# Down projection, token pairs 2 to 7: the second product moved to the end of the pair, and y's second half loaded in pieces of 128 tokens

## The chip, the cores and the metric

The kernel runs on one core of a Trainium2 chip. The metric is the device time of one execution in microseconds. Three executions of the kernel before took 781.5, 782.49 and 782.85 us; their median, 782.49 us, is the time before.

## The reference

A transformer block with modulation: a linear attention part and a gated feed-forward part, each with a residual. The change lies in the last matmul of the second, `@ w_down`.

```python
def _B_ref(x, w_gate, w_up, w_down):
    return _gelu(x @ w_gate) * (x @ w_up) @ w_down
x = A_x
mod = (_silu(c) @ w_mod).reshape(c.shape[0], 6, 1, -1)
...
x = x + ga * _A_ref(h, A_wqkv, A_wo)
h = _layernorm(x, axis=-1) * (1 + cb) + sb
x = x + gb * _B_ref(h, B_w_gate, B_w_up, B_w_down)
```

x has 2048 tokens of 1024 values, w_gate and w_up are 1024x3584, w_down is 3584x1024, all bf16. In the kernel y stands for `_gelu(x @ w_gate) * (x @ w_up)`, and the final line is out = x1 + gb * (y @ w_down), with x1 the result of the attention part.

## The kernel before, in words

**Recording and order.** Each instruction is recorded by `sch.op` or `sch.dma` with the byte ranges that it reads and writes in SBUF and in PSUM; from these the recorder derives what it must wait for, engine by engine, and emits semaphore waits. At the end `sch.reorder` rearranges the streams of VectorE (DVE), ScalarE (ACT) and GpSimd (POOL) by a table of costs and due times. The streams of TensorE (PE) and of SyncE (SP, which issues nearly all DMAs) keep the order in which they are written. DMAs of SP share 8 semaphore lanes in turn, and one waits for the one 8 before it.

**The down projection.** The 2048 tokens go in 8 pairs of token tiles, j = 0 to 7, of 2 x 128 tokens. The loop `for j in range(1, NP)` (L1917) handles j = 1 to 7, and `lastj` marks j = 7. For one pair, y (256 tokens by 3584) is held as two halves of the summation, `YL[0]` (`lo`) and `YL[1]` (`hi`), each of 14 chunks (k) of 128 by 256 tokens; w_down's columns are two halves of 512 (`BXT` and `STT`). The 2x2 block product (token tile s by column half c) is computed with seven products in place of eight, from sums and differences of the blocks. Each product is 14 matmuls of 128x128 by 128x512 (`dprod`, L1655, all issued on L1647):

- P1 and P2 take y's first token tile as it was loaded, in bf16: P1 from `YL[0]`, P2 from `YL[1]`.
- P5, P6, P7, P3 and P4 take sums of y blocks, in `XS[0]` or `XS[1]` (fp32r), and sums of weight blocks, prepared earlier (`TT`).
- `a_sum(i, k0, k1)` (L1627) makes the sums in two parts of 7 chunks: 0 writes XS[0] for P5, 1 writes XS[1] for P6, 2 writes XS[0] for P7, 3 writes XS[1] for P3 (it reads `YL[1]`, tokens 0 to 127), all on VectorE; 4 copies `YL[1]`, tokens 128 to 255, to XS[0] for P4, on ScalarE.

**PSUM.** Four banks for a pair, and the other four for the next (t = j % 2): `BA`, `BE`, `BB`, `BC` (L1406).

- P1 starts BA; `dpcp` (L1678, ScalarE) copies BA to BB; P2 adds to BA, which then holds output block 0 (tile 0, columns 0 to 511).
- P5 starts BE; `descp` (ScalarE) copies BE to `ES[0]` in SBUF.
- P6 adds to BB; `dpadd(j, BC)` (L1686, VectorE) writes BC = BB + ES[0]; P3 adds to BC: output block 1.
- P7 adds to BB; `dpadd(j, BE)` writes BE = BB + ES[0]: output block 2.
- P4 adds to BB: output block 3.

The order of TensorE in a pair is P1, P5, P6, P2, P7, P3, P4.

**Leaving PSUM.** `devac(j, n)` (L1706) finishes output block n: one VectorE op multiplies the bank by gb (L1714), one adds x1 from a slot in SBUF (L1715), and SP writes the slot to the output (L1716). `x1_load(j, n)` (L1699) has loaded that slot; there are 7 slots, and block n of pair j uses slot (4j+n) % 7.

**Loads of y.** `y_load(j, l, k0, k1, s0, s1)` (L1621) loads half l of pair j from DRAM (`scr_y`), chunks k0 to k1 and tokens s0 to s1 (all 256 unless given). Each half has a single buffer, so a load waits for every reader of what it overwrites. In SP's order of pair j come y_load(j+1, 0) after a_sum 2, and y_load(j+1, 1) in two parts of 7 chunks, each behind its part of a_sum 4.

Of the kernel before, what the change touches and what calls it, by code (L numbers as in the profile page):

```python
# [10 lines left out]
P = 128  # L11
# [53 lines left out]
NKP = NFP  # L65
NST = 14
# [284 lines left out]
def bass_adaLN_cond__linear_attn_block__geglu_ffn__prompt_kernel(  # L351
# [18 lines left out]
    with ExitStack() as es:  # L370
# [175 lines left out]
        def r_yl(l, k0=0, k1=NKP, s0=0, s1=256):  # L546
            if s1 - s0 == 256:
                return [(OFF_YL[l] + k0 * 512, OFF_YL[l] + k1 * 512, f"yl{l}")]
            return [(OFF_YL[l] + k * 512 + s0 * 2, OFF_YL[l] + k * 512 + s1 * 2, f"yl{l}") for k in range(k0, k1)]

        def r_xq(i, k0, k1):
            return [(OFF_XS[i] + k0 * 512, OFF_XS[i] + k1 * 512, f"xs{i}")]

        def r_bx(k, l0=0, l1=2):
            return [(PB[k] + l0 * 1024, PB[k] + l1 * 1024, f"bx{k}")]
# [4 lines left out]
        def r_bt(k, i):  # L560
            return [(PT[k][i], PT[k][i] + 2048, f"bt{k}_{i}")]

        def r_slot(i):
            return [(OFF_SLOT[i], OFF_SLOT[i] + 1024, f"x1s{i}")]
# [11 lines left out]
        def pr(b):  # L576
            return [(b * 2048, (b + 1) * 2048)]

        def PS(b, c0=0, c1=512):
            return ps_all[:, b * 512 + c0: b * 512 + c1]  # L580
# [1040 lines left out]
        def y_load(j, l, k0=0, k1=NKP, s0=0, s1=256):  # L1621
            sch.dma(Q, lambda e: e.dma_start(YL[l][:, k0:k1, s0:s1], scr_y[j // 4, :, j % 4, l, k0:k1, s0:s1]), wr=r_yl(l, k0, k1, s0, s1),
                    deps=o_y[j // 4], note=f"yl{j}.{l}.{k0}.{s0}", overwrite_ok=True)
# [19 lines left out]
        def dmm(b, fresh, lhs, rhs, note, c0=0, c1=512):  # L1643
            pend_ = None
            n = len(lhs)
            for i, ((l_, rl), (r_, rr)) in enumerate(zip(lhs, rhs)):
                pend_ = sch.op(T, lambda e, l_=l_, r_=r_, i=i: e.matmul(PS(b, c0, c1), l_, r_, start=fresh and i == 0, stop=i == n - 1, skip_group_check=True),  # L1647
                               rd=rl + rr, pwr=(pr(b) if i == 0 else ()), note=f"{note} {i}", overwrite_ok=True)
            if pend_ is not None:
                pset_writer(b, pend_)  # L1650

        def ya(l, s, k):
            return YL[l][:, k, s * P:(s + 1) * P], r_yl(l, k, k + 1, s * P, (s + 1) * P)

        def dprod(j, i, k0, k1, n=512):  # L1655
            t, ks = j % 2, range(k0, k1)
            if i in (1, 2):
                lhs = [ya(i - 1, 0, k) for k in ks]
                rhs = [(BXT[k][:, i - 1, :], r_bx(k, i - 1, i)) for k in ks]
            else:  # L1660
                xi, ti = {5: (0, 0), 6: (1, 1), 7: (0, 2), 3: (1, 3), 4: (0, 4)}[i]
                lhs = [(XS[xi][:, k, :], r_xq(xi, k, k + 1)) for k in ks]
                rhs = [(TT[k][ti][:, 0:n], r_bt(k, ti)) for k in ks]
            b = {1: BA, 2: BA, 5: BE, 6: BB, 7: BB, 4: BB, 3: BC}[i] + t
            dmm(b, i in (1, 5) and k0 == 0, lhs, rhs, f"down j{j} P{i}", 0, n)
# [12 lines left out]
        def dpcp(j):  # L1678
            t = j % 2
            sch.op(A, lambda e: e.activation(PS(BB + t), PS(BA + t), ACTF.Copy), prd=pr(BA + t), pwr=pr(BB + t), note="pcp")  # L1680

        def descp(j):
            t = j % 2
            sch.op(A, lambda e: e.activation(ES[0][:, :], PS(BE + t), ACTF.Copy), prd=pr(BE + t), wr=r_2k(OFF_ES[0], "es0"), note="escp")

        def dpadd(j, dst):  # L1686
            t = j % 2
            sch.op(V, lambda e: e.tensor_tensor(PS(dst + t), PS(BB + t), ES[0][:, :], ALU.add), prd=pr(BB + t), rd=r_2k(OFF_ES[0], "es0"),
                   pwr=pr(dst + t), note="padd")

        def t4_gate(k):
            sch.op(V, lambda e: e.tensor_tensor(TT[k][4][:, :], TTF[k][4][:, :], GB16[:, 0:512], ALU.mult), rd=r_bt(k, 4) + R_GB16, wr=r_bt(k, 4), note=f"t4g{k}")

        def tok(j):
            return (j // 4) * 8 + 2 * (j % 4)
# [3 lines left out]
        def x1_load(j, n):  # L1699
            s, c = TORD[n]  # L1700
            i = (4 * j + n) % 7
            c_ = tok(j) + s
            sch.dma(Q, lambda e: e.dma_start(SLT[i][:, :], scr_x1[c_, :, c * 512:(c + 1) * 512]), wr=r_slot(i), deps=[o_x1[c_ // 4]],
                    note=f"x1l{c_}.{c}", overwrite_ok=True)

        def devac(j, n, c0=0, c1=512, b=None):  # L1706
            s, c = TORD[n]
            i, c_ = (4 * j + n) % 7, tok(j) + s
            if b is None:
                b, p0, p1 = ((BA, BC), (BB, BE))[s][c] + j % 2, c0, c1  # L1710
            else:
                p0, p1 = 0, c1 - c0
            rng = [(OFF_SLOT[i] + c0 * 2, OFF_SLOT[i] + c1 * 2, f"x1s{i}")]
            sch.op(V, lambda e: e.tensor_tensor(PS(b, p0, p1), PS(b, p0, p1), GB16[:, c * 512 + c0:c * 512 + c1], ALU.mult), prd=pr(b), pwr=pr(b), rd=R_GB16, note=f"x2a {j}.{n}")  # L1714
            sch.op(V, lambda e: e.tensor_tensor(SLT[i][:, c0:c1], PS(b, p0, p1), SLT[i][:, c0:c1], ALU.add), prd=pr(b), rd=rng, wr=rng, note=f"x2b {j}.{n}")  # L1715
            sch.dma(Q, lambda e: e.dma_start(out_v[:, c_, c * 512 + c0:c * 512 + c1], SLT[i][:, c0:c1]), rd=rng, note=f"out{c_}.{c}.{c0}")  # L1716

        def rest_gate(j):
            b, i = BB + j % 2, (4 * j + 3) % 7
            sch.op(V, lambda e: e.tensor_tensor(PS(b), PS(b), GB16[:, 0:512], ALU.mult), prd=pr(b), pwr=pr(b), rd=R_GB16, note="u3g")  # L1720
            for h in range(2):
                d, p0, p1 = BB + (j + h) % 2, h * 256, h * 256 + 256
                sch.op(V, lambda e, d=d, p0=p0, p1=p1: e.tensor_tensor(PS(d, p0, p1), PS(b, p0, p1), SLT[i][:, p0:p1], ALU.add),
                       prd=pr(b), pwr=pr(d), rd=r_slot(i), note=f"u3x{h}")
# [107 lines left out]
        for n in range(7):  # L1832
            i, j = divmod(n, 2)
# [31 lines left out]
        H = (NST + 1) // 2  # L1865
        NP = S // 256

        def halves(i):
            a_sum(i, 0, H)
            a_sum(i, H, NST)  # L1870
# [46 lines left out]
        for j in range(1, NP):  # L1917
            lastj = j == NP - 1
            dprod(j, 1, 0, NST)
            dpcp(j)  # L1920
            if j == 1:
                devac(0, 0)
            else:
                halves(0)
                halves(1)
                devac(j - 1, 3)
            x1_load(j, 3)
            dprod(j, 5, 0, NST)
            descp(j)
            halves(2)  # L1930
            if lastj:
                for k in range(H, H + 4):
                    t4_gate(k)
            if not lastj:
                y_load(j + 1, 0)
            if j == 1:
                devac(0, 1)
            dprod(j, 6, 0, NST)
            dpadd(j, BC)
            halves(3)  # L1940
            if j == 1:
                devac(0, 2)
            dprod(j, 2, 0, NST)
            devac(j, 0)
            if lastj:
                for k in range(H + 4, NST):
                    t4_gate(k)
            if not lastj:
                x1_load(j + 1, 0)
            dprod(j, 7, 0, NST)  # L1950
            dpadd(j, BE)
            a_sum(4, 0, H)
            if not lastj:
                y_load(j + 1, 1, 0, H)
            a_sum(4, H, NST)
            if not lastj:
                y_load(j + 1, 1, H, NKP)
            devac(j, 2)
            if j == 1:
                devac(0, 3)  # L1960
            if not lastj:
                x1_load(j + 1, 1)
            if lastj:
                dprod(j, 3, 0, H - 1)
                dprod(j, 4, 0, H)
                rest_gate(j)
                dprod(j, 3, H - 1, NST)
                devac(j, 1)
                for h in range(2):
                    last_half(j, h)  # L1970
                continue
            dprod(j, 3, 0, NST)
            devac(j, 1)
            if not lastj:
                x1_load(j + 1, 2)
            dprod(j, 4, 0, NST)


        sch.reorder(mark[0], mark[1], (DVE_, ACT_, POOL_), {id(x4_op): 8.0})
# [73 lines left out]
```

## Time and profile before

| | |
|---|---|
| median of three runs | 782.49 us |
| the profiled execution: time / span | 781.51 us / 779.5 us |
| TensorE busy | 769.2 us, 99% of the span |
| VectorE, ScalarE, GpSimd busy | 656.8, 340.1, 47.6 us |
| down projection, one pair (j = 4, P1 to P1) | 22.04 us: TensorE busy 21.94, VectorE 15.25, ScalarE 3.09 |
| granted TensorE clock | 1.00 |
| y loads of 448 KB, from issue to landing | 4.1 us (median of 12) |
| output writes of 128 KB, from issue to landing | 1.7 us (median of 31) |

The profile is of one execution. Its span runs from the first instruction to the last; its time also holds what lies around them. PE is TensorE's matmuls and PEld its weight loads, which run under the matmul before. A matmul's recorded duration is longer than its distance to the next, since matmuls are pipelined; start-to-start distances are the better measure. A row "A <- B: 20.1, 11, 2.2" says that engine and line A stood idle until B released it, 20.1 us in 11 waits, the longest 2.2. Lines of a timeline give the start and the duration in us, the engine, the line, what is written and read, how many instructions are merged in the row, and in brackets the idle time ahead and what ended it.

### The profile page before, as it was taken

The numbers are of one execution on the slowest core, as the hardware profiler recorded it, in microseconds if no ns is written. First come the engines' busy times: TensorE is split into PE (matmuls) and PEld (weight loads), VectorE is DVE, ScalarE is ACT, GpSimd is POOL, SyncE is SP. The second block draws the span as 40 slices with busy tenths as digits, with TensorE's granted clock in tenths as the row PEclk, the third lists the DMA queues.
The fourth block names the chain that finished last, engine by engine and source line by source line (L and its number), as shares of the span: only waits on it lengthen the run. The fifth ranks groups of instructions, "written<-read, shape, count | busy, mean of one in ns | idle before, by whom it ended". The sixth has DMA issues, their size and how long they took to land.

```text
span 779.5 us, 10982 instructions
## 1 busy us (share of the span) xinstructions
PE 769.2 (99%) x3784; PEld 503.2 (65%) x3847; DVE 656.8 (84%) x1121; ACT 340.1 (44%) x566; POOL 47.6 (6%) x126
## 2 busy tenths in 40 slices
PE   8999999999999999999999999999999999999998
PEld 4444445666445676767676776767676676677766
DVE  6699989797698978897899989898889987676777
ACT  2497732211474577766654445444543211111111
POOL 2031300000230011100000000000000000000000
PEclk9999999999999999999999999999999999999999
DMA  9789759826697077847436475646545553344341
GB/s 290 250 170 250 158 93 250 230 69 123 137 247 190 28 206 239 226 116 185 132 111 172 126 207 188 198 118 195 148 123 151 157 171 119 120 142 135 115 135 40
DMA packets 209846, 125.92 MB, mean 162 GB/s; under 512 B 70528, under 2 KB 199424, under 8 KB 209792
## 3 DMA queue, kind: packets, MB, share of 16 engines
q1 hardware_dynamic: 209632, 125.16, 59.9%
q8 instruction: 30, 0.49, 0.3%
q14 instruction: 24, 0.20, 0.1%
q10 hardware_dynamic: 160, 0.07, 0.0%
HBM read 88.35 MB, written 23.22 MB: 143 GB/s over the span
## 4 chain that ended last, share of the span: by engine, by line
PE 91%; DVE 3%; SPq 3%; DMA 2%; issue 1%; ACT 0%; DVEq 0%; ACTq 0%
PE ps_all L1434 45%; PE ps_all L1647 23%; PE ps_all L944 7%; PE ps_all L1264 7%; PE ps_all L893 5%; PE ps_all L908 4%; SPq L631 1%; SPq L636 1%; DVE acc L844 1%; DMA wk<-in_A_wqkv_dram 1%; DVE acc L830 1%; DMA h1T<-xh 0%; DMA scr_row<-qt 0%; DMA mtb<-mb 0%; DVE w L1201 0%
## 5 line engine op out<-in xcount | busy, mean ns | idle before, releaser
L1434 PE MATMUL ps_all<-ss,tp 128*128 128x512 f32 x896 | 214.7, 396 | 0.0
L1434 PEld LDWEIGHTS ps_all<-ss,tp 128*128 128x128 f32 x896 | 168.1, 188 | 38.3 <-DVE ps_all L1446 0.6
L1647 PE MATMUL ps_all<-bt,xs 128*128 128x512 f32 (+1 forms) x552 | 130.2, 393 | 0.1
L1647 PEld LDWEIGHTS ps_all<-bt,xs 128*128 128x128 f32 x552 | 102.8, 188 | 23.3 <-issue 0.5
L1446 DVE TENSOR_TENSOR ps_all<-ps_all,es 128x512 f32<-128x512 f32 x112 | 77.6, 697 | 38.0 <-PE ps_all L1434 34.3
L1451 ACT ACTIVATE ge<-ps_all 128x512 f32<-128x512 f32 x112 | 64.1, 598 | 90.0 <-DVE ps_all L1446 46.1
L1402 DVE TENSOR_TENSOR tp<-wt 128x512 fp32r<-128x512 bf16 x112 | 74.4, 686 | 2.1 <-DMA wt<-in_B_w_gate_dram 1.5
L1455 DVE TENSOR_TENSOR yr<-ge,ps_all 128x512 bf16<-128x512 f32 x112 | 74.3, 683 | 1.5 <-PE ps_all L1434 0.9
L1402 DVE TENSOR_TENSOR tp<-wt,tp 128x512 fp32r<-128x512 bf16 x112 | 74.3, 685 | 0.0
L893 PE MATMUL ps_all<-wk,h1T 128*128 128x512 bf16 x239 | 55.3, 379 | 1.4 <-DVE h1T L757 0.8
L944 PE MATMUL ps_all<-h1T,wq 128*128 128x512 bf16 x256 | 56.7, 379 | 0.0
L1264 PE MATMUL ps_all<-w,pq 128*128 128x512 bf16 x252 | 55.9, 379 | 0.3
L1434 PE MATMUL ps_all<-ar,tp 128*128 128x512 f32 x224 | 55.3, 389 | 0.0
L882 ACT ACTIVATE eb<-ps_all 128x512 f32<-128x512 f32 x64 | 36.4, 594 | 39.0 <-PE ps_all L893 16.8
L1647 PE MATMUL ps_all<-bx,yl 128*128 128x512 bf16 x217 | 52.2, 380 | 0.8
L1434 PE MATMUL ps_all<-h20a,wt 128*128 128x512 bf16 x210 | 47.9, 379 | 0.9
L1434 PE MATMUL ps_all<-h21a,wt 128*128 128x512 bf16 x210 | 47.8, 379 | 1.0
L1434 PEld LDWEIGHTS ps_all<-ar,tp 128*128 128x128 f32 x224 | 42.0, 188 | 8.7
L1443 ACT ACTIVATE es<-ps_all 128x512 f32<-128x512 f32 x56 | 33.5, 600 | 30.8 <-PE ps_all L1434 30.8
L1440 ACT ACTIVATE ps_all<-ps_all 128x512 f32<-128x512 f32 x56 | 32.6, 582 | 30.6 <-PE ps_all L1434 30.3
L944 PEld LDWEIGHTS ps_all<-h1T,wq 128*128 128x128 bf16 x256 | 24.9, 98 | 30.0
L1264 PEld LDWEIGHTS ps_all<-w,pq 128*128 128x128 bf16 x256 | 24.8, 98 | 30.1 <-issue 0.5
(143 smaller groups left out, 880.8 us busy)
## 6 DMA issues: line engine op xcount, KB each, us to landing
wt<-in_B_w_gate_dram SPq DMA_DIRECT2D x28, 512.0 KB, 4.1
wt<-in_B_w_up_dram SPq DMA_DIRECT2D x28, 512.0 KB, 5.1
scr_y<-yr SPq DMA_DIRECT2D x56, 256.0 KB, 4.9
yl<-scr_y SPq DMA_DIRECT2D x8, 896.0 KB, 4.7
wmst<-in_w_mod_dram SPq DMA_DIRECT2D x6, 1024.0 KB, 6.8
yl<-scr_y SPq DMA_DIRECT2D x12, 448.0 KB, 4.1
wmq<-in_w_mod_dram SPq DMA_DIRECT2D x8, 512.0 KB, 7.6
rb<-scr_rd SPq DMA_DIRECT2D x32, 128.0 KB, 3.0
```

The lines of the kernel that those rows point to most:

```text
L882: sch.op(A, lambda e: e.activation(EB[i][:, :], PS(bank), ACTF.Exp), prd=pr(bank), wr=rng, note=f"{note}.exp")
L893: o = sch.op(T, lambda e, dc=dc: e.matmul(PS(bank), H1[sg][:, ci, dc, :], W_[:, dc, jg * 512:(jg + 1) * 512], start=(dc == 0), stop=(dc == ...
L944: o = sch.op(T, lambda e, dc=dc: e.matmul(PS(b), WQ[:, dc, qc * P:(qc + 1) * P], H1[sg][:, :, dc, :], start=(dc == 0), stop=(dc == NDC - 1 ...
L1264: last[half] = sch.op(T, lambda e, g=g, half=half: e.matmul(PS(b0 + half), PQ[sg][:, g, ci * P:(ci + 1) * P], W2[:, g, half * 512:(half + ...
L1402: sch.op(V, lambda e, t=t: e.tensor_tensor(TP[k][:, t, :, :], in0[:, t, :, :], in1[:, t, :, :], ALU.subtract), rd=r0[t:t + 1] + (r1[t:t + ...
L1434: o = sch.op(T, lambda e, l_=l_, r_=r_, dc=dc: e.matmul(PS(b), l_, r_, start=fresh and dc == 0, stop=dc == ND2 - 1, skip_group_check=True) ...
L1440: sch.op(A, lambda e: e.activation(PS(BB + t), PS(ba + t), ACTF.Copy), prd=pr(ba + t), pwr=pr(BB + t), note="pcp")
L1443: sch.op(A, lambda e: e.activation(ES[t][:, :], PS(be + t), ACTF.Copy), prd=pr(be + t), wr=r_2k(OFF_ES[t], f"es{t}"), note="escp")
L1446: sch.op(V, lambda e: e.tensor_tensor(PS(dst + t), PS(BB + t), ES[t][:, :], ALU.add), prd=pr(BB + t), rd=r_2k(OFF_ES[t], f"es{t}"), pwr=pr ...
L1451: sch.op(A, lambda e: e.activation(GE[i][:, :], PS(b), ACTF.Gelu_apprx_tanh), prd=pr(b), wr=r_2k(OFF_GE[i], f"ge{i}"), note="gelu")
L1455: sch.op(V, lambda e: e.tensor_tensor(YR[:, 2 * (v % 2) + l, h * SGW:(h + 1) * SGW], GE[i][:, :], PS(b + 1), ALU.mult), rd=r_2k(OFF_GE[i], ...
L1647: pend_ = sch.op(T, lambda e, l_=l_, r_=r_, i=i: e.matmul(PS(b, c0, c1), l_, r_, start=fresh and i == 0, stop=i == n - 1, skip_group_check ...
```

## The change

For j = 1 to 6 (the second to the seventh pair):

- P2 moves from between P6 and P7 to the end of the pair, behind P4. On TensorE the order is then P1, P5, P6, P7, P3, P4, P2, followed by the next pair's P1. Both P2 and P1 are bf16 products.
- `devac(j, 0)`, which needs P2, moves into the next pair, behind `devac(j, 3)` and ahead of `x1_load(j+1, 3)`, which uses the slot that it frees.
- y's second half of the next pair is loaded in three DMAs in place of two: tokens 128 to 255 at the two old places, tokens 0 to 127 (all 14 chunks) at the end of the pair, behind P2, which reads the old ones.

Pair 7 keeps P2 and its devac where they were, and so does pair 0, which lies outside the loop.

```diff
@@ for j in range(1, NP)
                 halves(0)
                 halves(1)
                 devac(j - 1, 3)
+                devac(j - 1, 0)
             x1_load(j, 3)
             dprod(j, 5, 0, NST)
             descp(j)
...
             if lastj:
                 for k in range(H, H + 4):
                     t4_gate(k)
-            if not lastj:
+            else:
                 y_load(j + 1, 0)
...
             halves(3)
             if j == 1:
                 devac(0, 2)
-            dprod(j, 2, 0, NST)
-            devac(j, 0)
             if lastj:
+                dprod(j, 2, 0, NST)
+                devac(j, 0)
                 for k in range(H + 4, NST):
                     t4_gate(k)
-            if not lastj:
+            else:
                 x1_load(j + 1, 0)
             dprod(j, 7, 0, NST)
             dpadd(j, BE)
             a_sum(4, 0, H)
             if not lastj:
-                y_load(j + 1, 1, 0, H)
+                y_load(j + 1, 1, 0, H, P, 2 * P)
             a_sum(4, H, NST)
             if not lastj:
-                y_load(j + 1, 1, H, NKP)
+                y_load(j + 1, 1, H, NKP, P, 2 * P)
             devac(j, 2)
...
             dprod(j, 3, 0, NST)
             devac(j, 1)
-            if not lastj:
-                x1_load(j + 1, 2)
+            x1_load(j + 1, 2)
             dprod(j, 4, 0, NST)
+            dprod(j, 2, 0, NST)
+            y_load(j + 1, 1, 0, NKP, 0, P)
```

## The prediction

> **What bounds the kernel now.** I read the busy table and the chain of waits first, then the table of who waited for whom (for TensorE over the whole run, for all engines over the down projection), then one token pair in order of time.
>
> From the page:
>
> ```profile
> PE 769.2 (99%) x3784; PEld 503.2 (65%) x3847; DVE 656.8 (84%) x1121; ACT 340.1 (44%) x566; POOL 47.6 (6%) x126
> ...
> PE 91%; DVE 3%; SPq 3%; DMA 2%; issue 1%; ACT 0%; DVEq 0%; ACTq 0%
> ```
>
> Who waited, TensorE alone, whole run:
>
> ```profile
> PE ps_all L661 <- POOL bmask L614: 2.1, 1, 2.1
> PE ps_all L893 <- DVE h1T L757: 0.8, 2, 0.5
> PE ps_all L801 <- DMA wmq<-in_w_mod_dram: 0.4, 1, 0.4
> PE ps_all L893 <- DMA wk<-in_A_wqkv_dram: 0.3, 1, 0.3
> ```
>
> Who waited, all engines, from 600 us to the end:
>
> ```profile
> ACT ps_all L1680 <- PE ps_all L1647: 56.6, 8, 8.3
> ...
> DVE ps_all L1688 <- PE ps_all L1647: 20.1, 11, 2.2
> DVE xs L1641 <- PE ps_all L1647: 6.4, 16, 0.5
> ...
> PEld ps_all L1647 <- issue: 4.4, 16, 0.5
> ```
>
> TensorE sets the end, and in the down projection (L1647) it waits for nobody: every line of the last table but one has another engine waiting for it. So nothing can be won there by relieving VectorE or a load; only shorter TensorE work counts, and any new TensorE wait is paid in full, since no later TensorE wait could absorb it. The "issue" rows are weight loads behind a change of operand type, looked at below.
>
> Pair j=4 in order of time (P1 starts at 688.23, the next P1 at 710.27; 22.04 us for 98 matmuls):
>
> ```profile
> 691.07 6.75 PE L1647 MATMUL ps_all<-bt,xs 128*128 128x512 f32 x28
> ...
> 697.65 2.71 PEld L1647 LDWEIGHTS ps_all<-bx,yl 128*128 128x128 bf16 x14 [0.26 <-issue]
> 697.66 3.19 PE L1647 MATMUL ps_all<-bx,yl 128*128 128x512 bf16 x13
> 697.92 0.70 DVE L1688 TENSOR_TENSOR ps_all<-ps_all,es 128x512 f32<-128x512 f32 x1 [2.15 <-PE ps_all L1647]
> 698.53 2.08 DVE L1641 TENSOR_TENSOR xs<-yl,xs 128x896 fp32r<-128x896 bf16 x2
> 700.50 9.92 PE L1647 MATMUL ps_all<-bt,xs 128*128 128x512 f32 x42
> ```
>
> The x28 is P5 and P6, the bf16 x13 (one record missing) is P2, the x42 is P7, P3, P4. The addition at 697.92 (L1688, dpadd) starts when P6 has ended. It reads the bank into which P6 and P7 both accumulate, BB+t; so it must be over before P7's first matmul, and it lies wholly under P2.
>
> **The change part by part.** One term gains, one costs, the rest is covered.
>
> *Two changes of operand type fewer in each of six pairs.* Spaced start to start, bf16 matmuls take 0.2158 us and f32 ones 0.2267 us in their steady run. 28 x 0.2158 + 70 x 0.2267 = 21.91 us, against 22.04 us measured: 0.13 us a pair are left for four changes (bf16 to f32 twice, f32 to bf16 twice). With P2 beside the next P1 two remain: gain 0.065 us a pair, 6 x 0.065 = 0.4 us. That is all that there is to gain; the 0.26 us of "issue" is idle time of the weight load under a running matmul, not of the matmuls.
>
> *P7 directly behind P6.* The program's order of VectorE is asum 2, dpadd(j, BC), asum 3, as before, and P7's first matmul still carries a wait on VectorE. Without P2 between, dpadd is bare. The step goes: P6's last matmul starts at 697.43 in the trace; dpadd starts at 697.92, 0.49 later (the same op behind P7, with f32 matmuls following, starts 0.43 later: 703.69 to 704.12); it takes 0.70; then TensorE must be let go and refill. That last part the down projection never shows, but one place before it does (late in the gate and up stage):
>
> ```profile
> 593.36 1.29 DVE L1446 TENSOR_TENSOR ps_all<-ps_all,es 128x512 f32<-128x512 f32 x2
> ...
> 594.10 1.23 PEld L1434 LDWEIGHTS ps_all<-ss,tp 128*128 128x128 f32 x6 [0.46 <-DVE ps_all L1446]
> ```
>
> There the same kind of addition ends at 594.05, the weight load it held starts 0.05 later, and the second matmul starts 0.34 after the first (594.105 to 594.442) in place of 0.227. So from P6's last start to P7's second start: 0.49 + 0.70 + 0.05 + 0.34 = 1.58 us, or 1.52 with the 0.43; undisturbed it is 2 x 0.227 = 0.45. Stall 1.07 to 1.13, I take 1.10 us a pair, for j = 1 to 6: 6.6 us. (Pair 7 and pair 0 keep P2 between.) Bounds: not below 0.91, which is P6's last matmul to its recorded end (0.39) + 0.70 + 0.05 - 0.227 with dpadd starting at once and no refill; not above 1.32, if a weight load of 0.19 us (its row: 188 ns) is bare on top. For six pairs 5.5 to 7.9 us.
>
> The Trainium skill, PSUM — Partial Sum Buffer, section "PSUM bank collisions raise a hardware error", says that the chip itself does not hold a matmul back from a bank that VectorE reads, and that the program must guard by bank with semaphores; the program does, which is why the stall comes as a semaphore wait.
>
> *What is late next.* All behind P7 moves by the same 1.1 us. P3 needs asum 3 (VectorE, behind dpadd): in the trace its two parts end 2.8 us after P6's end (698.53 + 2.08 against 697.82), and P3 now comes 1.1 + 3.2 us after P6's end: covered by 1.5 us. P7 itself needs asum 2's second part, which ends 1.1 us after it can start at P5's end (694.68, 1.09 long: 695.77), 1.9 us ahead of 697.66. P4 needs dpadd(j, BE), which keeps P3 as cover (3.2 us against 0.43 + 0.70).
>
> *devac(j, 0), two VectorE ops of 0.70 and 0.69 us, into the next pair.* VectorE is busy 15.25 of 22.04 us in the window of this pair, so 1.4 us find room. Before asum 2 (held until P5 is half done, about 4.6 us into the pair) VectorE now has P4's asums done 3 us earlier than before, as P2 lies behind P4. In the last pair it gains these two ops too, at the same place.
>
> *Loads.* y's second half comes as three DMAs in place of two: tokens 128 to 255 in two pieces of 224 KB at the old places, tokens 0 to 127 as 448 KB when P2 has ended; SP issues six more, each some 0.3 to 0.6 us of its queue. The runs in DRAM shrink from 3584 B to 256 B. The trace's packet records have a median of 140 ns for 3584 B and 18 ns for 256 B: 0.039 against 0.070 ns per byte and engine. The late piece is 1792 packets, 112 per engine, 2.0 us where it would be 1.1; I take 4.1 us (the row of 448 KB) + 0.9 = 5 us from P2's end. Its first reader is asum 3, behind dpadd, some 10 us after that. In the queue it waits for P2's end with the outputs of devac(j, 3) and devac(j, 0), x1_load(j+1, 3) and the next first-half load behind it; the last can't go before asum 2 is done anyway (7.7 us into the pair; 695.86 in the trace). x1_load(j, 3) takes the slot of (j-1, 0), so it now waits for that output to land (1.7 us), again ahead of that load's time. The two early pieces follow asum 4 and land some 19 us into the pair; P5 of the next pair needs the sums from them at 26. All at 0, with 5 us of cover.
>
> The Trainium skill, DMA: Bandwidth & Descriptors, section "Specifications", gives 512 B as the least transfer at line rate; the packet records agree (1.8 times the time per byte at 256 B). By the page too the pieces are only slower, under the same cover.
>
> **Sum.** -0.4 + 6.6 = +6.2 us. The profiled execution took 781.51 us (span 779.5), which is 1 us under the median of the runs, 782.49. So 787.7 for the first, and 782.5 + 6.2 = **788.7 us** for the median (0.8% more).
>
> **The rivals.**
> - *The wait costs nothing*: if P7's first matmuls needed only asum 2 (done 1.9 us ahead), the two type changes alone would be left: 782.1 us, not slower. For it: before shows no such TensorE wait. Against: dpadd reads BB+t, P7 writes BB+t, and the order tells of a VectorE wait there. It decides if dpadd ended before P6's last matmul, which it can't, needing P6's sum. 4%.
> - *A kernel faster by over 1.6 us* would need a TensorE wait that goes; the table has none in this stage. 2%.
> - *The late 128-token piece becomes the wait*: if it landed over 10 us after P2's end, asum 3 and P3 would be late in six pairs. At 12 us, 2 us less 1.5 of cover each, +3 us: 792 us. For it: 256 B packets; against: twice the cover. 5%.
> - *The clock falls in the gaps.* 128x512 matmuls of the first microseconds, started 0.427 us apart, ran at half rate. A spell of 3 us at that rate would cost 1.4 us a pair, 8 more: 797 us. Against: after the 0.46 us hole at 594.10 the granted clock stays 1.00. 3%. (The Trainium skill, TensorE: Matmul & The Clock Gate, section "Part 1", asks for about 3.4 us without work; a hole of 1.1 us would not do it.)
> - Forecast as summed: 86%.
>
> **How the numbers follow.** The bounds of the stall give 782.5 - 0.4 + 5.5 = 787.6 and 790.0; with a median that moves by some 0.7 either way (781.5 to 782.85 in the runs) and part of the late load, the range is 786.8 to 790.9. What a measurement can tell from no change is about 0.2%, 1.6 us. Slower: 86 + 5 + 3 = 94%; same 4%; faster 2%.
>
> **What would show it.** Right: in six pairs a row "PEld L1647 <- DVE L1688" of some 0.8 to 1.0 us idle each, nothing of that kind in pairs 0 and 7; P1 to P1 at 23.1 us; "issue" rows at type changes halved; VectorE's asum 3 not waiting for a load. Wrong: no TensorE wait on L1688; or waits on the loads or on L1641; or a granted clock under 1 in these pairs.

## The result, and the profile after

| | before | after |
|---|---|---|
| median | 782.23 us (6 runs, 781.45 to 782.85) | 788.62 us (6 runs, 787.93 to 789.32) |
| profiled execution: time / span | 781.51 / 779.5 us | 787.93 / 785.9 us |
| one pair, P1 (j = 4) to the next P1 | 22.04 us | 23.13 us |
| first P5 of pair 1 to the last matmul | 151.70 us | 158.27 us |

The changed kernel takes 1.0084 times as long (95% interval 1.0071 to 1.0097): slower by 6.4 us; 788.7 was forecast. The last row of the table is called the stretch below. It is read from the starts of single matmuls in the trace, and leaves out the stages before the down projection: in these profiles the first P5 starts anywhere from 624.4 to 626.1 us, which alone blurs the spans by more than some effects here.

The page of the changed kernel, busy times, chain of waits by line, and the two costly groups of L1647 (matmuls and weight loads of the f32 products):

```profile
PE 775.0 (99%) x3847; PEld 502.7 (64%) x3847; DVE 656.3 (84%) x1121; ACT 340.1 (43%) x566; POOL 47.6 (6%) x126
...
PE ps_all L1434 45%; PE ps_all L1647 23%; PE ps_all L908 7%; PE ps_all L1264 7%; PE ps_all L944 7%; PE ps_all L893 6%; SPq L631 1%; DMA wmq<-in_w_mod_dram 1%; SPq L636 1%; DVE ps_all L1688 1%; PE ps_all L926 0%; PE ps_all L1199 0%; SPq L625 0%; PE ps_all L1222 0%; PE ps_all L979 0%
...
L1647 PE MATMUL ps_all<-bt,xs 128*128 128x512 f32 (+1 forms) x552 | 129.6, 392 | 5.2 <-DVE ps_all L1688 5.2
L1647 PEld LDWEIGHTS ps_all<-bt,xs 128*128 128x128 f32 x552 | 102.3, 188 | 30.0 <-DVE ps_all L1688 7.7
```

The first of the two rows of L1647 in the kernel before:

```profile
L1647 PE MATMUL ps_all<-bt,xs 128*128 128x512 f32 (+1 forms) x552 | 130.2, 393 | 0.1
```

L1688, dpadd, is new on the chain that ended last, with 1%, and the matmuls of L1647 have idle time ahead of them that they had not: 5.2 us in place of 0.1, all put down to L1688. The busy share is 99% in both kernels and shows nothing of it.

Who waited for whom in the changed kernel, from 600 us to the end:

```profile
PEld ps_all L1647 <- DVE ps_all L1688: 7.7, 6, 1.3
...
PE ps_all L1647 <- DVE ps_all L1688: 5.2, 6, 0.9
...
PEld ps_all L1647 <- issue: 2.8, 10, 0.5
...
DVE xs L1641 <- DMA yl<-scr_y: 0.4, 1, 0.4
```

Six waits of TensorE, one in each of pairs 1 to 6. The weight load's row counts from the end of the last weight load, the matmul's from the recorded end of the last matmul, which lies later than the point at which the next could have started. What a pair loses (1.13 us, worked out below) lies between the two, 1.28 and 0.86 us a wait. "issue" has 10 waits where it had 16: one change from f32 to bf16 fewer in each of six pairs.

Pair j = 4 of the changed kernel in order of time:

```profile
698.94 0.33 SPq L1622 DMA_DIRECT2D yl<-scr_y  x1
...
701.00 0.70 DVE L1688 TENSOR_TENSOR ps_all<-ps_all,es 128x512 f32<-128x512 f32 x1 [2.15 <-PE ps_all L1647]
701.61 2.08 DVE L1641 TENSOR_TENSOR xs<-yl,xs 128x896 fp32r<-128x896 bf16 x2
701.76 9.40 PEld L1647 LDWEIGHTS ps_all<-bt,xs 128*128 128x128 f32 x42 [1.28 <-DVE ps_all L1688]
701.76 9.82 PE L1647 MATMUL ps_all<-bt,xs 128*128 128x512 f32 x42 [0.86 <-DVE ps_all L1688]
```

dpadd runs from 701.00 to 701.70, and P7's first weight load starts at 701.76. VectorE's asum 3 follows it with no wait for a load, and the next first-half load, issued at 698.94, landed at 703.61, before its first reader, a sum of the next pair, starts at 710.13.

### The profile page after: what moved, and what is told of

Its sections match the earlier page's. It is cut to its first block, busy times and chain, and to the rows that moved or that the text cites. A ratio compares the mean times of both kernels' runs of the same rounds, so it can differ in the third digit from the quotient of the medians.

```text
span 785.9 us, 11052 instructions
## 1 busy us (share of the span) xinstructions
PE 775.0 (99%) x3847; PEld 502.7 (64%) x3847; DVE 656.3 (84%) x1121; ACT 340.1 (43%) x566; POOL 47.6 (6%) x126
## 4 chain that ended last, share of the span: by engine, by line
PE 96%; SPq 2%; DMA 1%; DVE 1%; issue 0%; DVEq 0%
PE ps_all L1434 45%; PE ps_all L1647 23%; PE ps_all L908 7%; PE ps_all L1264 7%; PE ps_all L944 7%; PE ps_all L893 6%; SPq L631 1%; DMA wmq<-in_w_mod_dram 1%; SPq L636 1%; DVE ps_all L1688 1%; PE ps_all L926 0%; PE ps_all L1199 0%; SPq L625 0%; PE ps_all L1222 0%; PE ps_all L979 0%
## 5 line engine op out<-in xcount | busy, mean ns | idle before, releaser
L1647 PE MATMUL ps_all<-bt,xs 128*128 128x512 f32 (+1 forms) x552 | 129.6, 392 | 5.2 <-DVE ps_all L1688 5.2
L1647 PEld LDWEIGHTS ps_all<-bt,xs 128*128 128x128 f32 x552 | 102.3, 188 | 30.0 <-DVE ps_all L1688 7.7
L893 PE MATMUL ps_all<-wk,h1T 128*128 128x512 bf16 x248 | 56.9, 379 | 0.2 <-DVE h1T L757 0.2
L1647 PE MATMUL ps_all<-bx,yl 128*128 128x512 bf16 x230 | 52.3, 379 | 0.0
L1434 PE MATMUL ps_all<-h20a,wt 128*128 128x512 bf16 x224 | 51.0, 380 | 0.0
L1434 PE MATMUL ps_all<-h21a,wt 128*128 128x512 bf16 x224 | 50.9, 380 | 0.0
```

The costliest lines, as they stand in the source:

```text
L893: o = sch.op(T, lambda e, dc=dc: e.matmul(PS(bank), H1[sg][:, ci, dc, :], W_[:, dc, jg * 512:(jg + 1) * 512], start=(dc == 0), stop=(dc == ...
L1434: o = sch.op(T, lambda e, l_=l_, r_=r_, dc=dc: e.matmul(PS(b), l_, r_, start=fresh and dc == 0, stop=dc == ND2 - 1, skip_group_check=True) ...
```

## The experiments

Each kernel ran beside the kernel before on the same chip; times are medians, with the ratio to it. "Stretch" is the quantity of the table, in the profiled execution (before 151.70, after 158.27).

| kernel | time, ratio with 95% interval | stretch, us | one of pairs 2 to 5, us |
|---|---|---|---|
| changed kernel | 788.62, 1.0084 (1.0071 to 1.0097) | 158.27 | 23.13 |
| p2_back | 782.60, 1.0005 (0.9996 to 1.0015) | 151.93 | 22.04 |
| cover_2 | 786.40, 1.0059 (1.0039 to 1.0079) | 155.46 | 22.67 |
| cover_6 | 781.78, 0.9997 (0.9988 to 1.0006) | 151.71 | 22.04 |
| short_add | 786.49, 1.0055 (1.0040 to 1.0070) | 155.88 | 22.73 |
| late_1 | 788.20, 1.0073 (1.0057 to 1.0088) | 158.27 | 23.13 |
| late_2 | 797.63, 1.0195 (1.0181 to 1.0209) | 167.20 | 24.9 |
| split_p5 | 783.27, 1.0010 (1.0002 to 1.0019) | 152.57 | 21.97 |
| split_p5b | 781.65, 0.9997 (0.9988 to 1.0006) | 151.37 | 21.97 |

**p2_back: the move of P2 alone undone.**

```diff
+            if not lastj:
+                dprod(j, 2, 0, NST)
             if lastj:
                 dprod(j, 2, 0, NST)
...
             dprod(j, 4, 0, NST)
-            dprod(j, 2, 0, NST)
             y_load(j + 1, 1, 0, NKP, 0, P)
```

> P2 stands between P6 and P7 again for j = 1 to 6; the 128-token pieces of y and the devac moved into the next pair stay as in the changed kernel. Theory (P7 waits bare for dpadd, all else costs nothing): no TensorE wait on L1688, P1 to P1 at 22.04 us, 782.2 us, as before the change. Rival (the 256-byte pieces, the six DMAs more or the late devac cost the time): stays near 788.6 us. Mixed: in between, by the share that the loads have.

The time can't be told from that of the kernel before, the waits of pairs 1 to 6 on L1688 are gone, and a pair takes 22.04 us. So the six DMAs more, the 256-byte pieces and the late devac cost nothing in pairs 1 to 6. 0.23 us of the stretch remain, all in pair 7, where the first weight load of P4 comes late, behind the 14 of P7 and six of P3 (the 20 of the first row); this was not in the forecast:

```profile
766.68 4.54 PEld L1647 LDWEIGHTS ps_all<-bt,xs 128*128 128x128 f32 x20
...
770.40 0.95 ACT L1635 ACTIVATE xs<-yl 128x896 fp32r<-128x896 bf16 x1 [0.65 <-PE ps_all L1647]
770.76 0.69 DVE L1688 TENSOR_TENSOR ps_all<-ps_all,es 128x512 f32<-128x512 f32 x1
...
771.57 0.53 PEld L1647 LDWEIGHTS ps_all<-bt,xs 128*128 128x128 f32 x3 [0.35 <-ACT xs L1635]
```

The row puts the wait down to ScalarE's second copy (L1635), but that ended at 771.35, and in the kernel before the same weight load starts at 771.17, before its second copy has ended (771.27). What ended last is dpadd(7, BE), at 771.45: it reads BB, to which P4 adds. It runs some 0.4 us later behind P7's start than in the kernel before, because VectorE has the two ops of devac(6, 0) to do early in pair 7 (from 759.14) and is busy without a pause from there on. So the moved devac does cost 0.23 us here, by a wait of the same kind as the one that the change made. In the changed kernel VectorE makes the first sums of pair 7 under P2 of pair 6, is idle for 1.68 us ahead of asum 2, and pair 7 shows no such wait. (This is read from the timelines; no run tested it alone.)

**cover_2 and cover_6: how much of P2 is needed between P6 and P7** (the diff is cover_2's; cover_6 has 6 in place of 2).

```diff
+            if not lastj:
+                dprod(j, 2, 0, 2)
             if lastj:
                 dprod(j, 2, 0, NST)
...
             dprod(j, 4, 0, NST)
-            dprod(j, 2, 0, NST)
+            dprod(j, 2, 2, NST)
```

> For j = 1 to 6 the first 2 of P2's 14 matmuls stand between P6 and P7, the other 12 at the end of the pair. Theory: P7's second matmul still starts 1.59 us after P6's last, and 2 x 0.216 us of work now lie in that time: P1 to P1 at 23.13 - 0.43 = 22.70 us, 8 x 0 + 6 x 0.66 = +4.0 over 782.2: 786.2 us. Rival (the loss goes with how much of P2 stands at the end of the pair): 12/14 of 6.4 us, 787.7 us.

> For j = 1 to 6 the first 6 of P2's 14 matmuls stand between P6 and P7, the other 8 at the end of the pair. Theory: 6 x 0.216 = 1.30 us is more than the 1.13 us of the stall, so the wait on L1688 goes altogether; four changes of operand type a pair as before the change; P1 to P1 at 22.04 to 22.06 us, 782.2 us. Rival (the loss goes with how much of P2 stands at the end): 8/14 of 6.4 us, 785.9 us.

The timeline of cover_2 in pair j = 4:

```profile
700.17 0.61 PE L1647 MATMUL ps_all<-bx,yl 128*128 128x512 bf16 x2
700.44 0.70 DVE L1688 TENSOR_TENSOR ps_all<-ps_all,es 128x512 f32<-128x512 f32 x1 [2.15 <-PE ps_all L1647]
701.19 9.40 PEld L1647 LDWEIGHTS ps_all<-bt,xs 128*128 128x128 f32 x42 [0.91 <-DVE ps_all L1688]
```

P7 is let go 0.05 us after dpadd's end (701.14), exactly as without cover; two matmuls of work have slid into the hole, and the pair is 0.46 us shorter, of which 0.43 is their length. With six, no wait on L1688 is left and the stretch is that of before to 0.01 us. What counts is not how much of P2 stands at the end of the pair (12 and 8 of 14 matmuls), but how much work stands behind P6, against a stall of 1.13 us: 0.43 us of it shortened the stall, 1.30 us removed it. Between two and six matmuls nothing was run.

**short_add: the same order, a shorter addition.**

```diff
-        def dpadd(j, dst):
+        def dpadd(j, dst, n=512):
...
-            dpadd(j, BC)
+            dpadd(j, BC, 512 if lastj else 128)
```

> The changed kernel with dpadd(j, BC) on 128 of the 512 columns for j = 1 to 6 (the other columns are left out, so output block 1 of these pairs lacks two products there). Theory: the wait lasts as long as this one addition; 512 columns take 0.70 us and 256 take 0.43 in the trace, so 128 take about 0.30, the stall falls by 0.40 us a pair to about 0.73, and the time by 2.4 us to 786.2 us. Rival (what P7 waits for is something else that ends then, a sum, a load or the bank itself): 788.6 us.

The timeline of short_add in pair j = 4:

```profile
700.81 0.30 DVE L1688 TENSOR_TENSOR ps_all<-ps_all,es 128x128 f32<-128x128 f32 x1 [2.15 <-PE ps_all L1647]
701.01 2.08 DVE L1641 TENSOR_TENSOR xs<-yl,xs 128x896 fp32r<-128x896 bf16 x2
701.16 9.40 PEld L1647 LDWEIGHTS ps_all<-bt,xs 128*128 128x128 f32 x42 [0.88 <-DVE ps_all L1688]
701.16 9.82 PE L1647 MATMUL ps_all<-bt,xs 128*128 128x512 f32 x42 [0.46 <-DVE ps_all L1688]
```

0.40 us off the addition takes 0.40 us off the matmuls' idle time (0.86 to 0.46) and off the pair (23.13 to 22.73). asum 3, which follows dpadd on VectorE, moves forward with it, but ends about 2 us after P7 has started (703.09 against 701.16), so the wait isn't for that. It is for this one instruction.

**late_1 and late_2: where the cover of the late 128-token piece ends** (late_2 has the two lines behind `y_load(j + 1, 0)`).

```diff
             x1_load(j, 3)
+            if j > 1:
+                y_load(j, 1, 0, NKP, 0, P)
             dprod(j, 5, 0, NST)
...
             dprod(j, 2, 0, NST)
-            y_load(j + 1, 1, 0, NKP, 0, P)
```

> The changed kernel with the load of tokens 0 to 127 of y's second half moved in SP's order from P2's end behind x1_load(j, 3) of the next pair, about 5 us later. Theory (the load has some 6 us of cover ahead of asum 3): it lands about 9.5 us after P1's start, asum 3 starts at 10.5, no cost: 788.6 us. Rival (the load is close to a wait, or part of the loss): +1 us a pair or more, 793 us and over.

> As late_1, but behind the next first-half load too, some 3 us later still and behind 896 KB in the DMA queues. Theory: it lands about 14 us after P1's start, asum 3's first part ends at 15.2 where P3 could start at 13.8: a wait of about 1.5 us in the five pairs j = 2 to 6 (pair 7 has P2 as cover): +7.5, 796 us, with a TensorE wait on L1641 or on a load. If it costs nothing, the cover was twice what I take it for: 788.6 us.

In late_1 the stretch is that of the changed kernel to 0.01 us. The piece lands about 9.5 us after P1's start and asum 3 starts at 10.5, as forecast; in one pair it landed at 11.1, and asum 3 waited 0.5 us for it, which TensorE did not feel. In late_2 the load became the wait; its table of who waited, from 620 us on:

```profile
DVE xs L1641 <- DMA yl<-scr_y: 19.8, 6, 4.0
...
PEld ps_all L1647 <- DVE xs L1641: 9.5, 5, 2.0
PEld ps_all L1647 <- DVE ps_all L1688: 7.7, 6, 1.3
PE ps_all L1647 <- DVE xs L1641: 7.4, 5, 1.6
```

A second set of five TensorE waits, behind sums that wait for the load, beside the six untouched ones of dpadd. They cost 8.9 us (167.20 - 158.27), 1.8 a pair, where 1.5 was expected. So the prediction's rival of the late piece that becomes the wait exists, when the piece is issued 8.2 us after P1's start in place of 0.5; the changed kernel keeps well clear of it. Pair 7 was spared because no first-half load stands ahead of its piece, which landed at 9.6 us, and not because of P2 as the expectation has it.

**split_p5: other work behind P6, P2 left beside P1.** Six matmuls of P5 stand behind P6, and what has to read BB at once is now a copy by ScalarE.

```diff
+        def dcopy(j):
+            t = j % 2
+            sch.op(A, lambda e: e.activation(PS(BC + t), PS(BB + t), ACTF.Copy), prd=pr(BB + t), pwr=pr(BC + t), note="pcp")
...
+        def dpadd_c(j):
+            t = j % 2
+            sch.op(V, lambda e: e.tensor_tensor(PS(BC + t), PS(BC + t), ES[0][:, :], ALU.add), prd=pr(BC + t), rd=r_2k(OFF_ES[0], "es0"),
+                   pwr=pr(BC + t), note="padd")
...
         NP = S // 256
+        NP5 = 8
...
-            dprod(j, 5, 0, NST)
-            descp(j)
-            halves(2)
+            if lastj:
+                dprod(j, 5, 0, NST)
+                descp(j)
+                halves(2)
+            else:
+                dprod(j, 5, 0, NP5)
+                a_sum(2, 0, H)
+                dprod(j, 6, 0, NST)
+                dcopy(j)
+                dprod(j, 5, NP5, NST)
+                descp(j)
+                a_sum(2, H, NST)
+                dpadd_c(j)
...
-            dprod(j, 6, 0, NST)
-            dpadd(j, BC)
+            if lastj:
+                dprod(j, 6, 0, NST)
+                dpadd(j, BC)
```

> P2 stays at the end of the pair, beside the next P1; the order for j = 1 to 6 is P1, first 8 matmuls of P5, P6, last 6 of P5, P7, P3, P4, P2. ScalarE copies BB to BC behind P6 (as dpcp does for BA), VectorE adds ES[0] to BC when P5 is done, under P7. Theory: P7 now waits for the copy alone (0.43 + 0.58 + 0.05 = 1.06 us behind P6's last start), and 6 f32 matmuls of P5 (1.36 us) lie over it, so the stall goes and the two type changes fewer are left: P1 to P1 at 21.95 to 22.0 us, 781.8 us, 0.3 us under the kernel before, too little for its time alone to tell. Rival (a wait of some kind comes with P2 at the end of the pair whatever stands between P6 and P7): 788 us.

Half a miss: pairs 2 to 6 take 21.97 us, as expected, but the kernel came out 1.0 us slower than before (ratio 1.0002 to 1.0019), and its stretch 0.87 us longer. The timeline of its pair 1 says why:

```profile
634.50 0.69 DVE L1723 TENSOR_TENSOR ps_all<-ps_all,gb 128x512 f32<-128x512 f32 x1
...
635.23 0.69 DVE L1724 TENSOR_TENSOR x1s<-ps_all,x1s 128x512 bf16<-128x512 f32 x1
635.84 2.08 DVE L1641 TENSOR_TENSOR xs<-yl,xs 128x896 fp32r<-128x896 bf16 x2
...
636.97 6.66 PE L1647 MATMUL ps_all<-bt,xs 128*128 128x512 f32 x28 [0.94 <-DVE xs L1641]
```

In pair 1 VectorE still finishes blocks of pair 0 (L1723 and L1724 are devac's two ops there); one of them stood ahead of asum 3, and P3, which comes without P2 ahead of it, waited. That pair takes 1.26 us more than the five behind it.

**split_p5b: pair 1 left in the old order** (the diff is against split_p5).

```diff
             lastj = j == NP - 1
+            old = lastj or j == 1
...
-            if lastj:
+            if old:
                 dprod(j, 5, 0, NST)
...
-            if lastj:
+            if old:
                 dprod(j, 6, 0, NST)
...
-            if lastj:
+            if old:
                 dprod(j, 2, 0, NST)
+            if lastj:
                 devac(j, 0)
...
             dprod(j, 4, 0, NST)
-            dprod(j, 2, 0, NST)
+            if not old:
+                dprod(j, 2, 0, NST)
             y_load(j + 1, 1, 0, NKP, 0, P)
```

> split_p5 for j = 2 to 6 alone; pair 1 keeps the order of the kernel before (P2 between P6 and P7). In split_p5, pair 1 lost 1.4 us to a new wait: VectorE still has a block of pair 0 to finish ahead of asum 3, and P3 came too early. Theory: that wait goes, pairs 2 to 6 take 21.97 us each in place of 22.04, the down projection is 5 x 0.066 = 0.33 us shorter than in the kernel before: 781.9 us beside 782.2, within what the timing can't tell from no change. Rival (splitting P5 or the copy costs in more places): 783 us as split_p5.

The stretch is 0.33 us shorter than before, as forecast to 0.01 us, with pairs 2 to 6 at 21.97 us, and TensorE waits for nobody there. Its ratio, 0.9997 (0.9988 to 1.0006), shows no difference from the kernel before; against the changed kernel it takes back the whole loss. The gain of 0.33 us is seen in the trace of one execution, alike in all five pairs, and is about half of what the interval of the times leaves open (0.7 us either way).

## Why the prediction was right

- **The mechanism** held: P7 waits for dpadd(j, BC) in pairs 1 to 6 and nowhere else. p2_back removes the wait by one edit, cover_2 and cover_6 fill it, short_add shortens it by what the addition is shortened. One sign was off in size: idle time of 0.8 to 1.0 us ahead of P7's weight load was named, and it was 1.28 (0.86 ahead of the matmul).
- **The stall**: 1.10 us a pair forecast. From P6's last start (700.51 in the pair shown of the changed kernel) to P7's second (702.10) it is 1.59, less the undisturbed 0.45, = 1.13 us, the upper of the two values that it was worked out from (both times are starts of single matmuls): dpadd starts 0.49 us after the start of P6's last matmul here too, so the row to use was the first one (P6), not the mean with P7's 0.43.
- **The type changes**: 0.065 us a pair forecast, and split_p5b has it (22.04 to 21.97). In the changed kernel only 0.04 came out (23.13 = 22.04 + 1.13 - 0.04): P7 no longer starts after bf16, but it starts after a halt, and behind a halt, as behind bf16, f32 matmuls first stand a little over 0.227 us apart. Behind the halt the next five distances are 0.228 to 0.236 us, together about 0.025 us over the steady distance, which is what is missing. The two terms were not independent.
- **The sum**: +6.2 forecast, +6.57 in the stretch, +6.4 in the medians. The two misses add up (0.2 us of stall more, 0.15 us of gain less, over six pairs). That the median itself, 788.62, lies only 0.1 us from the forecast is in part luck: the kernel before came out at 782.23 in six runs, not at the 782.49 from which the forecast was added up.
- **A reading**: the full form of the prediction's table of waits from 600 us on also has three rows in which ScalarE or VectorE wait for a DMA or for VectorE, so not every row but one is a wait for TensorE; none is a wait of TensorE's, and the conclusion stands.
- **The covers**: the late piece was taken as 5 us to landing; it took 3.9 us (median of 6), and asum 3 never waited for it. late_1 and late_2 bracket the cover: about 5 us later costs nothing, 3 more and a queue of 896 KB cost 1.8 us a pair. In pair 7 the two VectorE ops were put at nothing too. That holds in the changed kernel (its pair 7 is as long as before's), where VectorE has idle time to spare at this place, but not in p2_back, where they delay dpadd(7, BE) and cost 0.23 us.
- **The clock** as granted lay between 0.998 and 1.00 in every run, with holes of up to 1.6 us between TensorE's matmuls (late_2). That agrees with the Trainium skill (TensorE: Matmul & The Clock Gate, "Part 1"), which asks for some 3.4 us without work before the clock drops; holes that long were not tried.

## What to carry to other kernels

A product that stands between two others on the same PSUM bank may be there as cover: ask what another engine has to read from that bank between them, and price it as the time to the reader's start (0.49 us from the start of the last matmul), its length (0.70), the way back to TensorE (0.05) and the refill up to the second matmul (0.34), less the two undisturbed distances (0.45): here 1.13 us. The gain from fewer changes of operand type (0.03 us each) was far smaller than that here. If the bulk must move, leave just as much behind as covers the read: 6 matmuls of 14 did as well as all.

What moves with the product counts too. The two VectorE ops of the late devac cost nothing where VectorE has idle time, and 0.23 us in p2_back, where it has none. There the row of waits named ScalarE, and only the end times of the instructions showed that VectorE was last.

## What the runs showed of the hardware

- 448 KB in 256-byte packets landed 3.9 us after the issue (median of 6). In 3584-byte packets, in the kernel before, it took 4.1 us (median of 12: 3.6 for the first of a pair's two loads, 4.4 for the second, which overlaps it). So the packet records, with 1.8 times the time per byte, show little in the landing of this load. Over the down projection the DMA queues are busy for some 40% of the time in both kernels; in late_2, behind 896 KB, the same piece took 6.2 us. Whether free queues are what hides the packets' time was not tested.
- After a halt behind a semaphore, the first two f32 matmuls start 0.34 us apart, the next five distances are 0.228 to 0.236 us, then 0.227 steadily. Behind a change from bf16 it takes about nine distances, 0.232 us on average (pair 4 of the two kernels).
